# Splitting the weights of w_in again in the second and third pass, instead of storing them split

## The chip, the core and the metric

One core of one Trainium2 chip. The metric is device time in microseconds (us) of one execution of the whole program. The names of the engines are those of the profile: PE multiplies matrices (PEld is its weight load), DVE is VectorE, ACT is ScalarE, POOL is GpSimd, SP is SyncE, which here only issues DMAs.

## The reference, cut to what matters

Three blocks follow each other: an attention with mixed heads, a dense layer with a gate, and a soft mixture of eight experts. The change lies in the middle one, on 1792 tokens, with d_model 768 and d_ff 2048:

```python
x = attn_out.transpose(0, 2, 1, 3).reshape(B * S, H * D)
h = x @ w_in
g = h - np.tanh(h)
x = (g @ w_out).astype(np.float32)
```

The third block takes logits x @ phi of 32 slots, a softmax over the tokens and one over the slots, and runs eight experts (w1 768x1024, w2 1024x768) on the slots.

## The kernel before, in words

The middle block is stage 1 of `moe_and_slots`. It goes over the tokens in four passes of 512, 512, 512 and 256 (`PASS`), and in each pass over 16 units of w_in: a unit is the 768x128 piece of w_in whose 128 columns of h are made at once. So there are 64 steps, t = 0 to 63; step t belongs to pass t // 16 and unit t % 16. `LAST` is 48 (first step of the fourth pass), `HALVES` is 52, `THREE` is 54.

**The product.** `product(t)` (line 845) runs, for each of six slices c of 128 rows of d_model, three matmuls of 128x512: high part of w by high part of x, low part of w by high part of x, high part of w by low part of x. Each operand is kept as two numbers, a rounded high part and the remainder, so that three fast matmuls give nearly full float32 precision. A unit thus lies in SBUF as 128 x 2 x 2 x 384 floats (768 KB): index 1 is the half of d_model, index 2 is high (0) or low (1). The ring of units has four places, `unit(t)`; `load_w(t + 3)` is issued by SP at the start of step t and waits until the place is free, that is until product t - 1 has been read.

**Where the split comes from.** `split_w(t)` makes the two parts from an unsplit unit (384 KB, loaded into the place of the low part): ACT copies it rounded to the high part (line 792), then POOL subtracts this from it (line 793). In pass 1 (t below 16) all units come this way, from the DRAM scratch `wi`. `save_w(t)` then stores the split unit, 768 KB, to the DRAM scratch `wis` (line 806; from the ACT queue for t above 1). From t = 16 to t = 51, `load_w` fetches the split unit from `wis` (line 783), and neither ACT nor POOL does anything for it. From t = 52 on, units are loaded unsplit in two halves and split by `split_half` (lines 799 to 802).

**The gate.** `gate_act(t - 1)` is emitted at the start of step t. On ACT it makes, in this order, sq (line 865, from the product's PSUM bank hp), qd (866), then whatever is passed as `beside`, then g (871, tanh) and mk (872). `gate_first(t - 1)` and `gate_last(t - 1)` are five DVE operations: 876, 877, 884, 889 and 890, the last of which completes g. `turn_g(t - 2)`, hooked in front of slice c = 2 of product t, transposes the finished g of step t - 2 on PE (line 916, four matmuls), and ACT copies the result out (919, shown as quad or tq). Every fourth step, `logits` adds eight matmuls after the product (line 1000). Steps 1 to 5 of a pass also carry the slot softmax of the pass before: among others `gates_first` (three DVE operations, then an ACT exponential in line 1054) and `slot_sum` (16 matmuls, line 1082), which reads what 919 copied. In steps 8 to 13 of passes 2 and 3, `split_x` splits the next pass's tokens, one slice per step: an ACT copy (828) and a DVE subtraction (829).

**Queues.** The order is written out by hand, and each engine runs its instructions in that order. SP issues nearly all DMAs; the stores of line 806 are in the ACT queue between the ACT operations of a step. In pass 1 the steps also turn w_out (969, with copies 973 and 975), fold it with phi (981 to 991) and convert the last pieces of w_out from float64 on ACT, DVE and POOL (lines 50 to 71).

After pass 4 the experts follow, whose weights (1536 KB and parts of it) are loaded as places become free in the steps of passes 2 and 4 and after.

Of the kernel before, what the change touches and what calls it, by code (L numbers as in the profile page):

```python
# [9 lines left out]
FP32 = mybir.dt.float32  # L10
# [637 lines left out]
def moe_and_slots(tc, ident, xd, wi, wo, wo4, wis, consts, w1, w2, out, box):  # L648
    nc = tc.nc
    NT, DM = out.shape  # L650
    KD = DM // 128
    NF = len(wi)
# [23 lines left out]
    LAST = NST - NF  # L676
    THREE = LAST + 6
    HALVES = LAST + 4
# [11 lines left out]
    def bank(tag, shape, name):  # L690
        return bank_pool[tag].tile(shape, FP32, tag=tag, name=name)

    def r32(ap):
        return ap.bitcast(F32R)
# [12 lines left out]
    def unit(t):  # L707
        return ring[t % 4] if t < THREE else ring[(4, 0, 1)[(t - THREE) % 3]]
# [67 lines left out]
    def load_w(t):  # L776
        if t == THREE:
            ring.append(mem["tmp"].tile([128, RU], FP32, tag="gl", name="rg").rearrange(
                "p (m h i) -> p m h i", m=2, h=2))
        if t < NF or t >= HALVES:  # L780
            nc.sync.dma_start(out=unit(t)[:, :, 1], in_=wi[t % NF].rearrange("p (m i) -> p m i", m=2))
        else:
            nc.sync.dma_start(out=unit(t), in_=wis[t % NF])
# [3 lines left out]
            nc.sync.dma_start(out=unit(t)[:, m, 1], in_=wi[t % NF][:, m * HALF:(m + 1) * HALF])  # L787

    def split_w(t, eng):
        if t < NF:  # L790
            w = unit(t)
            nc.scalar.activation(out=r32(w[:, :, 0]), in_=w[:, :, 1], func=ACTF.Copy)
            eng.tensor_tensor(out=r32(w[:, :, 1]), in0=w[:, :, 1], in1=w[:, :, 0], op=ALU.subtract)  # L793

    def split_half(t, m):
        if HALVES <= t < NST:
            h, l = unit(t)[:, m, 0], unit(t)[:, m, 1]
            if m == 0:
                nc.vector.tensor_copy(out=r32(h), in_=l)  # L799
            else:  # L800
                nc.scalar.activation(out=r32(h), in_=l, func=ACTF.Copy)
            nc.gpsimd.tensor_tensor(out=r32(l), in0=l, in1=h, op=ALU.subtract)  # L802

    def save_w(t):
        if t < NF:
            (nc.scalar if t > 1 else nc.sync).dma_start(out=wis[t], in_=unit(t))

    def x_of(p, c, l):
# [42 lines left out]
    def temps_of(t):  # L851
        n = PASS[t // NF]
        if t < 2:
            part = [quad[:, i * n:(i + 1) * n] for i in range(4)]
            return part[0], part[1], part[2], part[3] if t else mem["g0"]
        i = (t - LAST) % 2 * n if t >= LAST else 0
        qd = mem["qe"] if t == LAST - 1 else mem["qd"]
        return mem["sq"][t], qd[:, i:i + n], mem["mk"][:, :n], g_of(t)

    def gate_act(t, beside=None):  # L860
        hp = hps[t]
        if t > 1:
            mem["sq"] = {t: bank(f"q{t % 2}", [128, PASS[t // NF]], "sq")}
        sq, qd, mk, g = temps_of(t)
        nc.scalar.activation(out=sq, in_=hp, func=ACTF.Square)  # L865
        nc.scalar.activation(out=qd, in_=sq, func=ACTF.Square, bias=tshift)
        if t >= LAST - 2:
            gate_poly(t)
        if beside:
            beside()  # L870
        nc.scalar.activation(out=g, in_=hp, func=ACTF.Tanh)
        nc.scalar.activation(out=mk, in_=sq, func=ACTF.Relu, bias=tlimit, scale=-1.0)  # L872

    def gate_poly(t):
        sq, qd, mk, g = temps_of(t)
        nc.vector.scalar_tensor_tensor(out=qd, in0=qd, scalar=TG_E, in1=sq, op0=ALU.add, op1=ALU.mult)  # L876
        nc.vector.scalar_tensor_tensor(out=qd, in0=sq, scalar=-TG_A, in1=qd, op0=ALU.add, op1=ALU.mult)
# [55 lines left out]
    def late_high(i):  # L933
        return mem["ex"][6].bitcast(I32).rearrange("p (n f) -> p n f", f=CV)[:, i]
# [26 lines left out]
    def load_o(f):  # L961
        if f < LATE:
            nc.sync.dma_start(out=mem["wo"][f % NG], in_=wo[f])
# [136 lines left out]
    def step(t):  # L1100
        b, f = divmod(t, NF)
        hooks = {}

        def on(c, fn, *a):
            hooks.setdefault(c, []).append(lambda: fn(*a))

        if t == LAST:
            mem["qe"] = keep.tile([128, TM], FP32, tag="et", name="qe")
        if 2 < t < THREE - 2:
            load_w(t + 3)  # L1110
        elif t >= THREE - 2:
            on(KD // 2, load_half, t + 3, 0)
            on(KD, load_half, t + 3, 1)
        for n, hf in pieces.get(t - 1, []):
            if hf:
                load_o(n + NG)
        if t > 2:
            split_half(t + 1, 0)
            gate_act(t - 1, lambda: split_half(t + 1, 1) if t >= NF else split_w(t + 1, nc.gpsimd))
        else:  # L1120
            split_w(t + 1, nc.gpsimd)
        u = t - 2
        ws = pieces.get(t, [])
        if ws:
            on(1, turn_w, *ws[0], 4 <= t <= len(late_w) + 4)
        if t > 2:
            on(1, gate_first, t - 1)
        on(5 if t == LAST + 1 else 4 if t > LAST + 2 else 2, turn_g, u)
        if ws:
            on(3 if t in folds else 5, turn_w, *ws[1], 4 <= t <= len(late_w) + 4)  # L1130
        if b == 0:
            on(1, save_w, t)
        if b and f == 1:
            on(3 if b < NPASS - 1 else 5, logits, b - 1, NQ - 1)
            on(4 if b < NPASS - 1 else 5, logits_out, b - 1)
        if b and f == 2:
            hooks[1] = [lambda: mix_t(b - 1), lambda: slot_exp(b - 1)] + hooks[1]
            on(3, mix_n, b - 1)
            on(KD, slot_run, b - 1)
            on(KD, gates_first, b - 1)  # L1140
        if b and f == 3:
            on(4, slot_turn, b - 1)
            on(KD, gates_last, b - 1)
        if b == NPASS - 1 and f in (3, 4):
            on(KD, slot_sum, b - 1, 2 * f - 6, 2 * f - 4)
        elif 0 < b < NPASS - 1 and f in (4, 5):
            on(3, slot_sum, b - 1, 2 * f - 8, 2 * f - 6)
        if t > 2:
            on(4, gate_last, t - 1)
        if 0 <= t - 2 < len(late_w):  # L1150
            late_load(t - 2)
        if 0 <= t - 4 < len(late_w):
            on(3, f64_abs, nc, late_high(t - 4), late_raw(t - 4))
            on(5, late_first, t - 4)
        if 0 <= t - 5 < len(late_w):
            on(5, late_last, t - 5)
        if 0 <= t - 6 < len(late_w):
            on(5, late_store, t - 6)
        if b + 1 < NPASS:
            if f == 6:  # L1160
                load_x(b + 1)
            if 8 <= f < 8 + KD:
                on(4, split_x, b + 1, f - 8, nc.vector if b else nc.gpsimd)
        if len(ws) > 2:
            on(KD - 1, turn_w, *ws[2])
        if t in folds:
            on(KD - 1, fold_first)
            on(KD, fold_last, folds[t])
        if u % NG == NG - 1 and u % NF < NF - 1:
            on(KD, logits, u // NF, u % NF // NG)  # L1170
        product(t, hooks)
        if b == 1 and f % 2 == 1 and f // 2 < NX:
            give(mem["ex"][f // 2], f // 2 == NX - 1)
        if b == 1 and f == NF - 1:
            give(mem["thp"].tile([128, EXB], FP32, tag="x1", name="ex"))
        if b == NPASS - 2 and f == NF - 1:
            mem["slow"] = True
            for l in range(2):
                give(xap.tile([128, EXB], FP32, tag=f"x{l}", name="ex"))
        if b == NPASS - 1:  # L1180
            if f == 3:
                give(rgp.tile([128, EXB], FP32, tag="rgs", name="ex"))
            if f == 4:
                firsts.close()
                zp = whole.enter_context(tc.tile_pool(name="m_z", bufs=1, reuse_waits="tile"))
                for i in range(2):
                    give(zp.tile([128, EXB], FP32, tag=f"z{i}", name="ex"))
            if f == NF - 2:
                load_piece(len(pending))
                give(rgp.tile([128, EXB], FP32, tag="rg", name="ex"))  # L1190
            load_piece(2 if f < 4 or f > NF - 3 else 1)
# [57 lines left out]
    for t in range(2, NST):  # L1249
        step(t)  # L1250
    t = NST
# [226 lines left out]
def fused_kernel(  # L1478
# [14 lines left out]
    nc = tc.nc  # L1493
    const = ctx.enter_context(tc.tile_pool(name="const", bufs=1))
    dram = ctx.enter_context(tc.tile_pool(name="xdram", bufs=1, space=bass.MemoryType.DRAM))
    ident = const.tile([128, 128], FP32, name="ident")
    make_identity(nc, ident)
    DM, FF = moe_w_in.shape
# [1 line left out]
    wi = [dram.tile([128, DM], FP32, tag=f"wi{f}", name=f"wi{f}") for f in range(FF // 128)]  # L1500
    wo4 = [dram.tile([128, 4 * DM], FP32, tag=f"wo{k}", name=f"wo{k}") for k in range(FF // 512)]
    wo = [wo4[f // 4][:, f % 4 * DM:(f % 4 + 1) * DM] for f in range(FF // 128)]
    wis = [dram.tile([128, 2, 2, DM // 2], FP32, tag=f"wis{f}", name=f"wis{f}") for f in range(FF // 128)]
    order = [(f, hf, o) for f in range(FF // 128) for hf in range(2) for o in range(2)]
    NSL = moe2_phi.shape[1]
    NG = 128 // NSL
# [62 lines left out]
```

## Time and profile before

| | us |
|---|---|
| runs shown: median (lowest to highest) | 881.85 (880.51 to 899.1) |
| the profiled execution's own time | 884.14 |
| its span, from the first to the last instruction | 882.4 |

| engine | busy us | share of the span |
|---|---|---|
| PE | 810.1 | 92% |
| ACT | 573.2 | 65% |
| DVE | 551.8 | 63% |
| POOL | 249.5 | 28% |

The DMAs move 224.53 MB in that execution (36.18 MB of them written to HBM). Stage 1 lies between about 440 and 774 us: pass 1 to 549, pass 2 to 639, pass 3 to 724, pass 4 to 774. A row of a timeline gives start, duration, engine, line, operation, what it writes and reads, a count, and in brackets how long the engine was idle before it and what ended that. A row of a group gives busy time, the mean of one in ns, and the idle time before them with what ended it.

### The profile page before, as it was taken

To read this page: it belongs to the slowest core of one execution; us is meant where nothing else is said; L and a number is where in the kernel's file an instruction comes from. 1 tells how busy PE (TensorE), PEld (TensorE's weight loads), DVE (VectorE), ACT (ScalarE), POOL (GpSimd) and SP (SyncE) were. 2 spreads that over 40 slices of the span, in tenths; PEclk is the share of its full clock that TensorE was granted. 3 is DMA by queue.
4 is the path that set the end of the run, shared out by engine and by line. 5 is a ranking of instruction groups with operands and counts; after the bars stand their busy time and mean duration, and the time that the engine had idled before them with its cause. 6 is when DMAs were issued, how large, how long until landed. Compare 5 with 4: busy or idle time off the path is not lost.

```text
span 882.4 us, 28630 instructions
## 1 busy us (share of the span) xinstructions
PE 810.1 (92%) x11780; PEld 578.4 (66%) x11780; DVE 551.8 (63%) x1168; ACT 573.2 (65%) x1358; POOL 249.5 (28%) x428
## 2 busy tenths in 40 slices
PE   8888998799888999999899999999999999999975
PEld 6456776577655776666676677667776786964422
DVE  5356766668756777888456975567765777830104
ACT  4686877778877788888666786546664666821103
POOL 5233343434433444454312552000000003700000
PEclk9899999999999999999999999999999999999988
DMA  9697788887898888885759985678755457999998
GB/s 178 180 223 212 199 240 232 228 222 202 231 242 232 226 224 248 247 251 188 245 195 355 348 292 214 221 308 319 292 215 178 147 186 255 308 348 415 424 393 316
DMA packets 131766, 224.53 MB, mean 254 GB/s; under 512 B 44852, under 2 KB 112436, under 8 KB 128052
## 3 DMA queue, kind: packets, MB, share of 16 engines
q1 hardware_dynamic: 129360, 211.68, 76.1%
q10 hardware_dynamic: 2276, 11.02, 3.1%
q8 instruction: 93, 1.52, 0.7%
q14 instruction: 37, 0.30, 0.1%
HBM read 147.96 MB, written 36.18 MB: 209 GB/s over the span
## 4 chain that ended last, share of the span: by engine, by line
PE 59%; DMA 17%; ACT 10%; DVE 7%; issue 4%; POOL 1%; SPq 0%; ACTq 0%; POOLq 0%; DVEq 0%
PE hp L845 21%; PE pm L313 7%; DMA D<-S 7%; DMA ex<-in_moe_w_dram 6%; PE vx L395 6%; PE sc L279 5%; PE tm L356 5%; ACT e L325 4%; DVE mx L317 3%; PE kx L236 2%; PE gt L916 2%; PE sp L1082 1%; ACT aT L370 1%; PE lgp L1000 1%; DVE xs L405 1%
## 5 line engine op out<-in xcount | busy, mean ns | idle before, releaser
L325 ACT ACTIVATE e<-pm,mx 128x448 f32<-128x448 f32 x184 | 116.2, 645 | 78.2 <-DVE mx L317 76.5
L317 DVE TENSOR_REDUCE mx<-pm 128x1 f32<-128x448 f32 x184 | 106.1, 618 | 81.2 <-PE pm L313 80.8
L845 PE MATMUL hp<-xa,rg 128*128 128x512 f32 x576 | 153.5, 407 | 2.2 <-POOL rg L793 2.2
L356 PEld LDWEIGHTS tm<-wk,e 64*56 64x56 f32 x5888 | 107.1, 130 | 51.8 <-issue 32.3
L313 PE MATMUL pm<-D,wpre 64*64 64x448 f32 (+1 forms) x736 | 112.5, 585 | 16.7 <-DMA D<-S 13.0
L845 PEld LDWEIGHTS hp<-xa,rg 128*128 128x128 f32 x576 | 103.2, 190 | 32.3 <-issue 10.5
L356 PE MATMUL tm<-wk,e 64*56 64x60 f32 x5888 | 110.6, 217 | 9.6 <-issue 9.0
L279 PE MATMUL sc<-khi,qT 64*120 64x448 f32 (+1 forms) x384 | 85.1, 397 | 14.6 <-DVE xs L405 10.3
L342 POOL TENSOR_SCALAR wk<-wpost,rv 128x60 f32<-128x60 f32 x184 | 89.7, 521 | 16.5 <-DVE rv L335 11.0
L287 ACT ACTIVATE S<-sc 120x448 f32<-120x448 f32 (+1 forms) x186 | 89.4, 566 | 5.5 <-PE sc L279 4.9
L395 PE MATMUL vx<-aT,vn 128*64 128x120 f32 (+1 forms) x1536 | 85.4, 265 | 2.0 <-ACT S L287 1.4
L331 POOL TENSOR_SCALAR rv<-ss 128x2 f32<-128x2 f32 x92 | 23.7, 258 | 223.3 <-ACT e L325 188.9
L802 POOL TENSOR_TENSOR rg<-rg 128x384 fp32r<-128x384 f32 x24 | 23.9, 1015 | 208.6 <-DVE rg L799 203.9
L876 DVE SCALAR_TENSOR_TENSOR qd<-qd,sq 128x512 f32<-128x512 f32 (+1 forms) x61 | 37.6, 617 | 69.9 <-ACT mk L872 64.7
L395 PEld LDWEIGHTS vx<-aT,vn 128*64 128x64 f32 x1536 | 75.9, 139 | 7.3 <-ACT S L287 3.6
L370 ACT ACTIVATE aT<-tm 128x480 f32<-128x480 f32 x144 | 76.2, 598 | 1.1 <-PE tm L356 1.1
L845 PE MATMUL hp<-xb,rg 128*128 128x512 f32 x288 | 74.7, 404 | 0.0
L865 ACT ACTIVATE sq<-hp 128x512 f32<-128x512 f32 (+1 forms) x62 | 32.9, 531 | 59.3 <-PE hp L845 59.2
L279 PEld LDWEIGHTS sc<-khi,qT 64*120 64x120 f32 (+1 forms) x384 | 46.8, 176 | 32.2 <-PE tm L356 10.8
L845 PEld LDWEIGHTS hp<-xb,rg 128*128 128x128 f32 x288 | 52.0, 188 | 16.6 <-issue 6.3
L71 POOL TENSOR_TENSOR fa<-fa,f 128x384 f32<-128x384 f32 x56 | 57.5, 1027 | 5.4 <-DVE f L66 1.1
L313 PEld LDWEIGHTS pm<-D,wpre 64*64 64x64 f32 (+2 forms) x736 | 25.6, 135 | 50.3 <-DMA D<-S 18.5
(197 smaller groups left out, 1399.9 us busy)
## 6 DMA issues: line engine op xcount, KB each, us to landing
ex<-in_moe_w_dram SPq DMA_DIRECT2D x21, 1536.0 KB
D<-S SPq DMA_DIRECT2D x144, 210.0 KB
rg<-wis SPq DMA_DIRECT2D x36, 768.0 KB
f<-in_moe_w_in_dram SPq DMA_DIRECT2D x32, 384.0 KB
wis<-rg ACTq DMA_DIRECT2D x14, 768.0 KB
f<-in_moe_w_out_dram SPq DMA_DIRECT2D x24, 384.0 KB
rg<-wi SPq DMA_DIRECT2D x19, 384.0 KB
wi<-fa SPq DMA_DIRECT2D x32, 192.0 KB
```

Source lines behind the costliest of these rows:

```text
L71: eng.tensor_tensor(out=out, in0=bits(a), in1=bits(p), op=ALU.add)
L279: nc.tensor.matmul(xs[e][0][:ni], lhsT=qT[n][s, l, p, :ni], rhs=kt[s], start=(i == 0), stop=(i == 2))
L287: nc.scalar.activation(out=dst, in_=xs[e][0][:ni], func=ACTF.Copy)
L313: nc.tensor.matmul(xs[x][64 * i:64 * i + 64], lhsT=wpre[k0:k1], rhs=d[i][k0:k1], start=True, stop=True)
L317: nc.vector.tensor_reduce(out=mx[:, x:x + 1], in_=xs[x], op=ALU.max, axis=AX.X, negate=True)
L325: nc.scalar.activation(out=es[x], in_=xs[x], func=ACTF.Exp, bias=mx[:, x:x + 1], accum_out=ss[:, x:x + 1])
L342: nc.gpsimd.tensor_scalar(out=wk, in0=wpost, scalar1=rv[:, x:x + 1], scalar2=None, op0=ALU.mult)
L356: nc.tensor.matmul(xs[i][64 * z:64 * z + JH, x, c], lhsT=es[x][h, j:j + JH], rhs=wks[x][h], start=True, stop=True)
L370: nc.scalar.activation(out=out[:, :, c0:c0 + m].rearrange("p a (x i) -> p a x i", x=2), in_=x, func=ACTF.Copy)
L395: nc.tensor.matmul(x[64 * e:64 * e + 64, i, :ni], lhsT=nat_v[b, h // NP][:, h % NP, c, :], rhs=a[:, c, h, :ni], start=(c == 0), stop=(c == ...
L845: nc.tensor.matmul(hp, lhsT=r32(w[:, m, hl, cs]), rhs=r32(x_of(b, c, l)), start=(c == 0 and i == 0), stop=(c == KD - 1 and i == 2))
L876: nc.vector.scalar_tensor_tensor(out=qd, in0=qd, scalar=TG_E, in1=sq, op0=ALU.add, op1=ALU.mult)
```

## The change

`load_w` fetches the unsplit 384 KB from `wi` for all steps below 48 (and from 52 on, as before); only steps 48 to 51 still fetch 768 KB from `wis`. `split_w` splits every unit below 48; in steps 15 to 46 it is what `gate_act` takes as `beside`, with POOL for the subtraction. `save_w` stores units 0 to 3 alone.

```diff
@@ load_w
-        if t < NF or t >= HALVES:
+        if t < LAST or t >= HALVES:
             nc.sync.dma_start(out=unit(t)[:, :, 1], in_=wi[t % NF].rearrange("p (m i) -> p m i", m=2))
         else:
             nc.sync.dma_start(out=unit(t), in_=wis[t % NF])
@@ split_w
-        if t < NF:
+        if t < LAST:
             w = unit(t)
             nc.scalar.activation(out=r32(w[:, :, 0]), in_=w[:, :, 1], func=ACTF.Copy)
             eng.tensor_tensor(out=r32(w[:, :, 1]), in0=w[:, :, 1], in1=w[:, :, 0], op=ALU.subtract)
@@ save_w
-        if t < NF:
+        if t < HALVES - LAST:
             (nc.scalar if t > 1 else nc.sync).dma_start(out=wis[t], in_=unit(t))
@@ step
-            gate_act(t - 1, lambda: split_half(t + 1, 1) if t >= NF else split_w(t + 1, nc.gpsimd))
+            gate_act(t - 1, lambda: split_half(t + 1, 1) if t >= LAST else split_w(t + 1, nc.gpsimd))
@@ fused_kernel
-    wis = [dram.tile([128, 2, 2, DM // 2], FP32, tag=f"wis{f}", name=f"wis{f}") for f in range(FF // 128)]
+    wis = [dram.tile([128, 2, 2, DM // 2], FP32, tag=f"wis{f}", name=f"wis{f}") for f in range(4)]
```

## Rows read from the trace of the kernel before

**Rows 1.** Windows by stage: stretch, us, busy time (instructions) per engine, granted clock, DMA share, GB/s

```profile
440.00:549.00 109.00, 103.30 (x680) 77.40 (x680) 75.74 (x132) 77.04 (x146) 39.42 (x27) 0.99 0.81 286
549.00:639.00 90.00, 89.53 (x458) 64.35 (x457) 59.71 (x99) 52.05 (x95) 0.00 (x0) 1.00 0.74 282
639.00:724.00 85.00, 84.87 (x432) 62.20 (x431) 58.80 (x100) 49.35 (x93) 0.00 (x0) 1.00 0.51 177
...
774.00:882.00 108.00, 88.47 (x743) 43.67 (x741) 21.77 (x58) 20.07 (x45) 2.32 (x8) 0.94 0.98 386
```

**Rows 2.** Timeline of pass 3, steps 39 to 41, ACT, DVE and PE

```profile
680.07 0.58 ACT L865 ACTIVATE sq<-hp 128x512 f32<-128x512 f32 x1 [2.16 <-PE hp L845]
...
681.23 0.60 PE L916 MATMUL gt<-ident,g 128*128 128x128 f32 x4
...
682.47 0.69 DVE L876 SCALAR_TENSOR_TENSOR qd<-qd,sq 128x512 f32<-128x512 f32 x1 [2.38 <-ACT mk L872]
...
684.62 0.58 ACT L865 ACTIVATE sq<-hp 128x512 f32<-128x512 f32 x1 [1.69 <-PE hp L845]
...
685.12 0.73 DVE L890 COPY_PREDICATED g<-mk,hp 128x512 f32<-128x512 int32 x1
...
686.00 0.63 PE L916 MATMUL gt<-ident,g 128*128 128x128 f32 x4
...
690.57 0.61 PE L916 MATMUL gt<-ident,g 128*128 128x128 f32 x4
```

**Rows 3.** Timeline of PE in pass 3, the transposes of steps 42 to 45

```profile
696.36 0.60 PE L916 MATMUL gt<-ident,g 128*128 128x128 f32 x4
...
700.91 0.60 PE L916 MATMUL gt<-ident,g 128*128 128x128 f32 x4
...
705.69 0.63 PE L916 MATMUL gt<-ident,g 128*128 128x128 f32 x4
...
710.27 0.60 PE L916 MATMUL gt<-ident,g 128*128 128x128 f32 x4
```

**Rows 4.** Timeline of pass 1, steps 10 to 12, where the split is made

```profile
511.72 1.84 POOL L793 TENSOR_TENSOR rg<-rg 128x768 fp32r<-128x768 f32 x1 [0.81 <-ACT rg L792]
...
516.31 0.58 ACT L865 ACTIVATE sq<-hp 128x512 f32<-128x512 f32 x1 [0.20 <-PE hp L845]
...
517.51 0.83 ACT L792 ACTIVATE rg<-rg 128x768 fp32r<-128x768 f32 x1
...
519.44 0.69 DVE L876 SCALAR_TENSOR_TENSOR qd<-qd,sq 128x512 f32<-128x512 f32 x1 [1.21 <-ACT mk L872]
```

**Rows 5.** Timeline of pass 2 around the slot softmax, steps 19 and 20

```profile
569.78 0.31 ACT L1054 ACTIVATE ceK<-ceK 128x128 f32<-128x128 f32 x1 [2.71 <-DVE ceK L1053]
...
575.04 0.74 DVE L890 COPY_PREDICATED g<-mk,hp 128x512 f32<-128x512 int32 x1
...
576.08 0.60 PE L916 MATMUL gt<-ident,g 128*128 128x128 f32 x4
...
577.79 0.62 PE L1082 MATMUL sp<-quad,es 128*32 128x512 f32 x2 [0.41 <-ACT quad L919]
```

**Rows 6.** Waits of SP's queue from 427 to 549 us: us in total, times, longest

```profile
SPq L781 <- DMA wis<-rg: 38.0, 9, 11.0
```

**Rows 7.** Timeline of pass 1, steps 8 and 9, ACT and PE

```profile
498.44 0.60 ACT L919 ACTIVATE quad<-gt 128x512 f32<-128x512 f32 x1 [0.93 <-DMA rg<-wi]
...
503.82 0.55 PE L969 MATMUL wt<-ident,ex 128*128 128x128 f32 x3 [0.59 <-ACT ex L973]
```

**Rows 8.** Timeline of pass 1: one DVE operation beside POOL and without it

```profile
500.24 1.28 POOL L829 TENSOR_TENSOR xb<-xb 128x512 fp32r<-128x512 f32 x1
...
500.56 1.17 DVE L54 TENSOR_SCALAR ex<-ex 128x384 f32<-128x384 f32 x1
...
516.03 0.34 DVE L54 TENSOR_SCALAR ex<-ex 128x384 f32<-128x384 f32 x1
```

**Rows 9.** One line, L829, subtraction of split_x: ns min/median/max, first and last start

```profile
L829 DVE TENSOR_TENSOR xa<-xa x12: 667/679/691, 438.4 to 629.4; 128x512 fp32r<-128x512 f32 x12
```


## Prediction

> **What bounds the kernel now.** I read the windows by stage first. In passes 2 and 3, the two stretches that the change alters most, PE is busy nearly all the time, 89.5 of 90 us and 84.9 of 85, at a granted clock of 1.00, POOL does nothing at all, and DMA is at 0.74 and 0.51 of its engines' time [rows 1]. So there is time on POOL, and DMA is not what these passes wait for; but a busy PE does not show how near the other engines are. For that I read the timeline of three plain steps of pass 3 [rows 2]. One product's gate goes: sq starts on ACT at 680.07, DVE's first operation (876) at 682.47, released by ACT's last one, mk (872), not by the qd that it reads; the last (890) ends at 685.12 + 0.73 = 685.85, and the transposes of this g start on PE at 686.00. Those transposes come two steps after the product that they belong to. The transposes of step 39 start at 681.23; then PE does the rest of product 39, whose sq starts at 684.62; so from one step's transposes to those two steps later there is a loop of 3.39 us (PE) + 5.93 us (680.07 to 686.00) = 9.32 us, and measured, 681.23 to 690.57, 9.34 us. PE's own work between two transposes is 4.55 us in a plain step (700.91 - 696.36) and 5.79 us where logits follow (696.36 - 690.57) [rows 2, 3]. Two plain steps are 9.10 us, less than 9.34: the loop over ACT and DVE already ends last once in four steps, and PE ends last in the others.
>
> That is the rule of this kernel: T(t), the start of the transposes in step t, is the later of T(t-1) + 4.55 (5.79 after logits) and T(t-2) + 9.34. From T(41) = 690.57 it gives 696.36, then 700.91, then 696.36 + 9.34 = 705.70 and 700.91 + 9.34 = 710.25; the rows have 705.69 and 710.27 [rows 2, 3]. Four steps are 19.70 us, 0.26 more than PE's work of 3 x 4.55 + 5.79 = 19.44.
>
> **The change part by part.**
>
> *The copy on ACT* (32 of them, steps 15 to 46) goes between qd and g, ahead of mk, which releases DVE. Pass 1 shows this very order: sq at 516.31, the copy at 517.51 for 0.83, and 876 at 519.44, again released by mk [rows 4]. From sq to 876 that is 3.13 us, against 2.40 in pass 3 [rows 2]. So a copy puts 0.73 us into the loop, and 9.34 becomes 10.07. What hides it is the slack of PE's bound, which is there in most steps. With T(41) = 0 the rule now gives 5.79; then 10.34 by PE (10.07 by the loop); then 15.86 by the loop (14.89 by PE); then 20.41 by both. Four steps are 20.41, 0.71 more than 19.70. So it costs 0.73 once where the loop ends last, not in every step. Walking through the 32 steps like this, there are five such places in the plain stretches: the transposes of steps 24, 28 and 32 in pass 2 and of 40 and 44 in pass 3. 5 x 0.73 = 3.65 us. If no slack hid it the price would be 32 x 0.73 = 23.4 us, and if DVE were not held by mk it would be 0; I take the walk, since its rule gives the rows of before to 0.02 us.
>
> *The steps around the slot softmax* have more PE work and mostly room for 0.73. There is one place in each pass where the delay counts twice: the exponential of 1054 waits on ACT for DVE, which does its part after 890, and the next sq stands behind it on ACT (569.78, idle 2.71 for DVE; there are two such rows, one in each pass) [rows 5]. A 890 that is 0.73 late makes that sq 0.73 late, and its gate gets a copy of its own: 1.46. In pass 2 the transposes of step 20 have 0.15 to spare (890 ends at 575.78, they start at 576.08, and 0.15 is the least gap in rows 2), so they come 1.31 later; but the slot sums behind them wait 0.41 for ACT in any case [rows 5], which takes about 0.4 back: 0.9. In pass 3, step 36, I find no such wait and no slack: 1.46. Together 2.4 us.
>
> *The subtraction on POOL*: 1.84 us, released by the copy [rows 4]. It ends 1.20 + 0.83 + 1.84 = 3.87 after sq, and the product that needs it starts at about the next sq, 4.55 later (684.62 - 680.07) [rows 2]. 0.7 us to spare, on an engine that was idle: nothing. If that cover went, each 0.1 us over would cost PE 0.1 us in that step. Bounds: 0, and, if all of PE's idle time in pass 1, 109.00 - 103.30 = 5.7 us [rows 1], were waits for the 13 subtractions that POOL makes there, 0.44 each, 32 x 0.44 = 14 us; I take 0, since the rows show when each one ends.
>
> *The loads* of units 16 to 47 halve, from 768 to 384 KB, 12.6 MB in all. SP issues them at the same places, two steps before ACT's copy reads them (before: three steps before PE did). Two steps are at least 9.1 us. What is queued ahead is at most one expert piece of 1536 KB, about 4 us at the 386 GB/s of the last stretch [rows 1]. They land in time, and nothing ended later for them in passes 2 and 3: 0 both ways. A copy whose load were late would hold tanh and mk behind it, and with them DVE and PE.
>
> *The stores* of units 4 to 15 go, 9.4 MB. In pass 1 SP's loads waited 38.0 us in nine waits for stores to leave a place of the ring [rows 6]. These loads are issued three steps early, so most of that is hidden. What I can follow to PE is one place: ACT idle for 0.93 before 498.44, the store in its queue waiting for a DMA, and PE then waiting 0.59 for ACT's copy in the next step [rows 7]. I take 0.7 us back. Bounds: 0, and all of PE's idle time there, the 5.7 us. I stay near the low end because the rest of that time includes waits on work that no store touches.
>
> *Pass 4 and after* are not edited. Their loads begin with the events of step 47, and from 774 us DMA is at 0.98 [rows 1]; a delay at step 47 is passed on whole, not absorbed, because these loads cannot start sooner.
>
> **Sum**: 3.65 + 2.4 - 0.7 = +5.3 us. The profiled execution took 884.14 us, its span 882.4 and 1.7 around it, and would become 889.4. It lies 2.3 us above the median of the runs shown, 881.85; from that median I predict 887.2 us (+0.6%).
>
> [...] In pass 1 DVE's line 54 took 1.17 us while POOL's line 829 ran (500.24 to 501.52), and ended 0.21 after it; alone it took 0.34 [rows 8]. [...]
>
> **The rivals.**
> 1. *Fewer bytes win.* SP's 38 us of waits were holding pass 1 more than I can follow, and all of PE's 5.7 us there go; this equals the loop's price of 6.0 less 0.3, so the time is about 882 (881.85 + 6.0 - 5.7), and about 876 if DVE were released before mk as well. For it: DMA is the only resource that gets lighter. Against it: passes 2 and 3 show no wait for DMA, and in pass 1 the same order of ACT held 876 to mk [rows 4]. It decides from 6 us of relief on: then not slower. Chance 0.16.
> 2. *The loop in every step.* If PE's bound gives less slack than the rule says, 32 x 0.73 - 0.7 = +22.7: 904.6. Against it: the rule gives the two rows that it was not read from to 0.02. Chance 0.04.
> 3. *POOL before DVE.* 829 runs 0.68 us in each of six steps of pass 2, and shorter, on half the columns, in six of pass 3 [rows 9]. It follows 890, so starts 0.73 + 5.78 = 6.51 after its step's sq, 0.7 to 1.96 after the next sq; POOL wants to start 2.03 after it. [...] Were POOL first, 829 would end 3.87 + 0.68 = 4.55 after sq and the 876 due at 3.13 would be 1.4 late: 12 x 1.4 = 17 us at most, 904 with the forecast. Chance 0.06.
> 4. *The change does less than it says*, for instance a unit still fetched split: 881.85. Nothing speaks for it. Chance 0.01.
>
> **How the numbers follow.** The forecast has 0.73. Its own range is 884 to 891, from the two ends of pass 1's gain that seem near and a repeat of the runs. For 8 in 10 it reaches down to the mild form of rival 1 and up to half of rival 3: 881 to 894. About 2% either way (864 and 899.5) is what a measurement of this kernel can tell from no change: faster than that 0.01, within 0.93, slower 0.06, from the full forms of rivals 2 and 3.
>
> **What would show it.** In the changed profile: 202.5 MB by DMA (224.53 - 12.6 - 9.4); line 792 48 times; in passes 2 and 3, 3.13 from sq to 876 in place of 2.40; transposes two steps apart by 10.07 where the loop ends last, four steps in 20.4; passes 2 and 3 together 6 us longer, pass 1 somewhat shorter, pass 4 and the tail as long as before. I am wrong if PE waits for POOL's 793 in passes 2 and 3, if 876 starts before mk ends, if DVE's 829 grows to over 2 us, if pass 1 loses more than 2 us, or if the tail changes its length.

## The result, and the profile after

The changed kernel takes 893.08 us (median of 6 runs), the kernel before, run beside it, 882.54 us (6 runs): a ratio of 1.0145, 95% interval 1.0101 to 1.019. The ratio is taken from fast runs alone, without the slowest of the kernel before, so it is above the quotient of the two medians, 1.0119. The change is thus inside 2%, but clearly a loss: 10.5 us by the medians (8.9 to 16.8 by the interval) where 5.3 were forecast. The time is inside the range of 881 to 894, outside the forecast's own 884 to 891. The profiled execution of the changed kernel took 888.63 us, with a span of 886.9.

The two profiled executions differ by only 4.5 us. A part of that lies ahead of the change: the first matmul of step 0 begins at 439.75 us before and at 436.01 after (from 431.64 to 440.10 in the profiles of all the kernels of this study), and steps 0 to 2 take 19.60 and 18.07 us; of the six profiled kernels built on the changed one three show the shorter value and three the longer. The granted clock tells the two apart. Windows from the first matmul of step 0, before and after (columns as in [rows 1]):

```profile
439.75:443.25 3.50, 3.50 (x39) 2.48 (x38) 1.77 (x3) 3.18 (x8) 0.00 (x0) 0.51 0.83 280
```

```profile
436.01:439.51 3.50, 3.50 (x79) 2.77 (x75) 1.76 (x3) 3.43 (x10) 0.00 (x0) 1.00 0.72 251
```

At a granted clock of 0.51 the first six matmuls of line 845 took 2.87 us together, at 1.00 they took 1.65. All nine profiles in which steps 0 to 2 take 19.6 us show this stretch, and none of the three in which they take 18.1; the change does not decide it. So I compare stretches, from the first matmul of a step (line 845) to the first one of a later step:

| stretch | before, us | after, us | difference | forecast |
|---|---|---|---|---|
| pass 1, steps 3 to 15 | 89.42 | 88.16 | -1.26 | -0.7 |
| passes 2 and 3, steps 16 to 47 | 175.01 | 186.75 | +11.74 | +6.05 |
| pass 4 | 50.70 | 50.53 | -0.17 | 0 |
| after pass 4 | 107.90 | 107.36 | -0.54 | 0 |

Within passes 2 and 3 the 11.7 us lie so: 6.9 in the plain stretches (forecast 3.65), 1.80 in step 20 and 2.18 in step 36 (forecast 0.9 and 1.46), 0.74 in step 16 (forecast 0). Four plain steps take 21.16 us in pass 2 and 21.07 in pass 3, against 19.83 and 19.68 before.

The page of the changed kernel, busy time of each engine and the DMA's volume:

```profile
PE 807.4 (91%) x11780; PEld 575.4 (65%) x11780; DVE 552.6 (62%) x1168; ACT 595.3 (67%) x1390; POOL 307.4 (35%) x460
...
DMA packets 134134, 202.51 MB, mean 228 GB/s; under 512 B 44660, under 2 KB 120436, under 8 KB 130420
```

The volume is the forecast one. The windows of passes 2 and 3 (columns as in [rows 1]):

```profile
542.00:637.00 95.00, 90.05 (x457) 63.93 (x456) 59.37 (x99) 63.22 (x111) 29.54 (x16) 1.00 0.55 199
637.00:729.00 92.00, 86.61 (x434) 62.23 (x433) 61.55 (x102) 60.00 (x107) 27.66 (x15) 1.00 0.34 108
```

DMA's share fell from 0.74 and 0.51 to 0.55 and 0.34, POOL has work now, and PE is idle for 4.95 and 5.39 us, where before it was idle for 0.5 and 0.1 [rows 1]. What PE waited for in these two passes (us in total, times, longest):

```profile
PE gt L916 <- DVE g L890: 5.6, 10, 0.8
PE gt L916 <- ACT qd L866: 2.4, 2, 1.2
PE sp L1082 <- ACT quad L919: 0.9, 1, 0.9
PE wt L969 <- DVE ex L975: 0.8, 1, 0.8
PE hp L845 <- POOL rg L793: 0.6, 1, 0.6
```

Together 10.3 us; before, the same view has one row, the 0.4 us for quad of [rows 5]. Ten of the waits are the transposes' for DVE's 890, the end of the gate. So in the plain stretches the gate is late ten times, not five: steps 24, 28, 32, 40 and 44, which the prediction named, are 0.53 to 0.73 us longer than before, and the step behind each (25, 29, 33, 41 and 45) another 0.62 to 0.69. Why, ACT's waits of the same stretch say:

```profile
ACT qd L866 <- DVE hp L889: 9.4, 16, 1.6
```

Line 866 writes qd, and there is one qd buffer: it must wait until line 889 of the previous gate has read it. Before, no such wait exists. But the trace of before shows how near it was. Timeline of the kernel before, pass 3, between the gates of [rows 2]:

```profile
680.68 0.69 ACT L866 ACTIVATE qd<-sq,tshift 128x512 f32<-128x512 f32 x1
...
684.40 0.69 DVE L889 SCALAR_TENSOR_TENSOR hp<-qd,hp 128x512 f32<-128x512 f32 x1
684.62 0.58 ACT L865 ACTIVATE sq<-hp 128x512 f32<-128x512 f32 x1 [1.69 <-PE hp L845]
685.23 0.69 ACT L866 ACTIVATE qd<-sq,tshift 128x512 f32<-128x512 f32 x1
```

889 is done at 685.09; 866 starts 0.14 later, on ACT's account alone, right behind sq. With some 0.09 from 889's end to an 866 that waits for it (693.30 to 693.39 below), qd could come round in 685.09 - 680.68 + 0.09 = 4.50 us, against a plain step of 4.55 on PE: 0.05 us of slack, which no wait shows. The changed kernel in pass 3, steps 41 to 44:

```profile
692.62 0.68 DVE L889 SCALAR_TENSOR_TENSOR hp<-qd,hp 128x512 f32<-128x512 f32 x1
693.33 0.73 DVE L890 COPY_PREDICATED g<-mk,hp 128x512 f32<-128x512 int32 x1
693.39 0.69 ACT L866 ACTIVATE qd<-sq,tshift 128x512 f32<-128x512 f32 x1 [0.41 <-DVE hp L889]
...
693.98 0.84 ACT L792 ACTIVATE rg<-rg 128x768 fp32r<-128x768 f32 x1
694.21 0.63 PE L916 MATMUL gt<-ident,g 128*128 128x128 f32 x4 [0.49 <-DVE g L890]
...
697.84 0.68 DVE L889 SCALAR_TENSOR_TENSOR hp<-qd,hp 128x512 f32<-128x512 f32 x1
...
698.62 0.69 ACT L866 ACTIVATE qd<-sq,tshift 128x512 f32<-128x512 f32 x1 [0.41 <-DVE hp L889]
...
703.39 0.58 ACT L865 ACTIVATE sq<-hp 128x512 f32<-128x512 f32 x1 [1.49 <-PE hp L845]
...
706.52 0.69 DVE L876 SCALAR_TENSOR_TENSOR qd<-qd,sq 128x512 f32<-128x512 f32 x1 [1.68 <-ACT mk L872]
```

From one 866 to the next, 693.39 to 698.62, is 5.23 us = 4.50 + 0.73. The copy lies inside this loop as it lies inside the transposes' loop, but this one closes in one step, the other in two: two rounds of qd are 10.46, more than the 10.07 of the transposes, so after the change qd ends last where plain steps follow each other. It makes the gate late in two of four steps; then the step with logits, 5.79 us on PE against 5.23, takes the delay up. Where 866 does not wait, sq to 876 is 3.13 (703.39 to 706.52), the forecast value.

With both loops in the rule (T(t), and the start of each 866 no earlier than 5.23 after the last one) four plain steps come to 21.08 by calculation; measured 21.07.

### The profile page after: what moved, and what is told of

It is laid out like the page before. It is cut to its first block, busy times and chain, and to the rows that moved or that the text cites. A ratio compares the mean times of both kernels' runs of the same rounds, so it can differ in the third digit from the quotient of the medians.

```text
span 886.9 us, 28736 instructions
## 1 busy us (share of the span) xinstructions
PE 807.4 (91%) x11780; PEld 575.4 (65%) x11780; DVE 552.6 (62%) x1168; ACT 595.3 (67%) x1390; POOL 307.4 (35%) x460
## 2 busy tenths in 40 slices
DMA packets 134134, 202.51 MB, mean 228 GB/s; under 512 B 44660, under 2 KB 120436, under 8 KB 130420
## 4 chain that ended last, share of the span: by engine, by line
PE 52%; DMA 14%; DVE 13%; ACT 12%; issue 6%; POOL 2%; SPq 0%; POOLq 0%; ACTq 0%; DVEq 0%
PE hp L845 14%; PE pm L313 7%; PE vx L395 7%; DMA ex<-in_moe_w_dram 6%; DMA D<-S 5%; PE sc L279 5%; PE tm L356 5%; DVE mx L317 3%; ACT e L325 3%; PE kx L236 3%; ACT rg L792 2%; PE gt L916 2%; PE sp L1082 1%; PE lgp L1000 1%; ACT S L287 1%
## 5 line engine op out<-in xcount | busy, mean ns | idle before, releaser
L793 POOL TENSOR_TENSOR rg<-rg 128x768 fp32r<-128x768 f32 x45 | 83.0, 1844 | 166.6 <-ACT rg L792 117.1
L313 PE MATMUL pm<-D,wpre 64*64 64x448 f32 (+1 forms) x736 | 110.5, 573 | 12.2 <-DMA D<-S 8.1
L71 POOL TENSOR_TENSOR fa<-fa,f 128x384 f32<-128x384 f32 x56 | 57.5, 1027 | 5.8 <-DVE f L66 1.5
L313 PEld LDWEIGHTS pm<-D,wpre 64*64 64x64 f32 (+1 forms) x736 | 25.3, 133 | 45.7 <-DMA D<-S 16.1
```

Of the source, the lines that this page charges most:

```text
L71: eng.tensor_tensor(out=out, in0=bits(a), in1=bits(p), op=ALU.add)
L313: nc.tensor.matmul(xs[x][64 * i:64 * i + 64], lhsT=wpre[k0:k1], rhs=d[i][k0:k1], start=True, stop=True)
```

## The experiments

Theory: the copy on ACT makes the loss, by the qd loop. Rivals: the transposes' loop alone; POOL's subtraction; the loads and stores. Ratios are to the kernel before, run beside it on the same chip.

**e2_copy_only and e3_pool_only**: the copy alone, and the subtraction alone, in the kernel before, each where the changed kernel has it (in e3 `beside` holds the second pair of lines in place of the first).

```diff
+    def beside(t):
+        if NF <= t < LAST:
+            h = r32(unit(t)[:, :, 0])
+            nc.scalar.activation(out=h, in_=bits(h), func=ACTF.Copy)
...
+            l = r32(unit(t)[:, :, 1])
+            nc.gpsimd.tensor_tensor(out=l, in0=bits(l), in1=unit(t)[:, :, 0], op=ALU.subtract)
```

> The kernel before, with one ACT copy of 128x768 put where the change puts its copy, in steps 15 to 46: it copies the high part of the next unit onto itself, so nothing computed changes, POOL does nothing more and all loads and stores stay as before. Theory (two loops over ACT and DVE: the transposes two steps on, and qd, the one buffer that line 889 of a gate must have read before line 866 of the next gate may write it, which makes qd to qd 4.51 us before and 5.24 with a copy of 0.73): passes 2 and 3, from the first matmul of step 16 to that of step 48, take 187 us as after the change, against 175.0 before; four plain steps 21.1, with waits of line 866 for line 889. One loop alone, as I forecast: 181, four plain steps 20.4. Rival, POOL or the unsplit loads make the second half of the loss: about 181 here. The total is 11 to 13 us over before by the theory, 6 by the others.

Measured: 893.1 us (4 runs), ratio 1.0153, interval 1.0086 to 1.0221. Passes 2 and 3 take 185.81 us, four plain steps 21.15 and 21.07. The waits of ACT and PE there (line numbers 9 higher):

```profile
ACT qd L875 <- DVE hp L898: 9.0, 16, 1.3
...
PE gt L925 <- DVE g L899: 5.6, 10, 0.8
```

The same sixteen and ten waits as in the changed kernel. So the copy alone makes 10.8 of the 11.7 us.

> The kernel before, with one POOL subtraction of 128x768 per step in steps 15 to 46, of the shape and in the place of the change's, but no ACT copy and the loads and stores of before. The low part of a unit in passes 2 and 3 becomes low minus high, which changes the values of the products there and not their number. Theory: nothing, passes 2 and 3 take 175.0 us within 0.5 and the total is that of before. Rival, POOL beside DVE's line 829 or late for PE: up to 5 us more, waits of PE for POOL, 829 over 1 us.

Measured: 881.2 us (10 runs), ratio 0.9969, interval 0.9923 to 1.0016; passes 2 and 3 take 175.14 us, 0.13 more than before. POOL alone costs nothing, as forecast.

**e1_two_qd**: a second qd buffer in the changed kernel. It lies where another tile is free, so it serves the odd gates from the sixth of a pass on; gates 16 to 20 and 32 to 36 have one buffer as before.

```diff
+    def second(t):
+        return NF <= t < LAST - 1 and t % 2 and t % NF >= 5
...
-        qd = mem["qe"] if t == LAST - 1 else mem["qd"]
+        qd = mem["qe"] if t == LAST - 1 else mem["qd2"] if second(t) else mem["qd"]
...
+        if NF <= t < LAST and f == 6:
+            mem["qd2"] = keep.tile([128, TM], FP32, tag="et", name="qd")
```

> The changed kernel with a second qd buffer for the odd steps from the sixth step of passes 2 and 3 on, so that line 866 need not wait for line 889 of the gate before it. Theory: the waits of 866 for 889 go there, four plain steps take 20.4 in place of 21.1, passes 2 and 3 take 183 to 184 us in place of 186.8, the total 3 to 4 us less than the changed kernel. Rival (the qd wait only shifts what PE waits for anyway): 186 to 187.

Measured: 890.0 us (9 runs), ratio 1.0093, interval 1.0065 to 1.0122. Four plain steps take 20.57 and 20.42 us, and the waits in passes 2 and 3 are now

```profile
ACT qd L869 <- DVE hp L892: 2.7, 2, 1.6
...
PE gt L919 <- DVE g L893: 3.6, 5, 0.8
```

This is the cleanest piece of evidence. With the qd loop gone from the plain stretches, what is left is what the prediction walked through: five late gates in place of ten, four steps of pass 3 in 20.42 where 20.41 was forecast. They lie in the very steps that it named, 24, 28, 32, 40 and 44, each 0.71 to 0.76 us longer than before, 3.63 together (forecast 3.65). The forecast's rule was right for the loop it knew. Passes 2 and 3 fall by 3.3 us to 183.45; steps 20 and 36, where qd still has one buffer, stay at 8.96 and 8.97.

**e8_two_copies**: e2 with its copy made twice.

```diff
             nc.scalar.activation(out=h, in_=bits(h), func=ACTF.Copy)
+            nc.scalar.activation(out=h, in_=bits(h), func=ACTF.Copy)
```

> The kernel before with two copies of 128x768 on ACT in the place where the change puts one, in steps 15 to 46, each of the next unit's high part onto itself. Theory: with 1.46 us more the loop over qd is 5.97 us and longer than any plain step of PE, and now ends last in each: four plain steps take 23.9 us (19.7 before, 21.1 with one copy). The transposes' loop alone would give 21.6. Rival (a copy costs the same each time): 22.5.

Measured: 920.82 us (a single run). Four plain steps take 23.21, 24.41, 23.29 and 24.39 us, mean 23.8; the rule with both loops gives 23.9, with the transposes' loop alone 21.6, and the same price for each copy 22.5. Passes 2 and 3 are 34.4 us over before; 7.1 of these lie in step 20, where PE's granted clock was 0.50 over 6.80 us (last section). From one 866 to the next it is now 6.10 us (623.15 to 629.25), and four such rounds are 24.40, what the later fours take. The second copy adds 0.87 to the round, 3.5 in four steps, and 2.7 of these are paid: past its slack, the loop hands on most of what is put into it.

**e4_stores_kept**: the changed kernel with all sixteen units stored.

```diff
-        if t < HALVES - LAST:
+        if t < NF:
             (nc.scalar if t > 1 else nc.sync).dma_start(out=wis[t], in_=unit(t))
```

> The changed kernel with all 16 units stored as before (the twelve stores of pass 1 come back; nobody reads those twelve). Theory: steps 3 to 15, from the first matmul of step 3 to that of step 16, take 89.4 us as before, against 88.2 after the change, most of it in step 9 (11.7 against 10.8), where ACT's queue waits; passes 2 and 3 stay at 187. Rival (pass 1 is shorter by chance, or by what came before it): 88.2.

Measured: 896.02 us (a single run). Steps 3 to 15 take 89.39 us, as before the change (89.42). SP's waits for stores in pass 1, first in the changed kernel and then in this one:

```profile
SPq L781 <- DMA wis<-rg: 9.6, 3, 6.7
```

```profile
SPq L781 <- DMA wis<-rg: 42.5, 10, 10.9
```

Against 38.0 before [rows 6]. The stretch as a whole does not show that pass 1 gained by the stores, since its step 3 varies by itself: 6.60 us here, 7.60 before, 7.16 in the changed kernel, and 9.64 in e1, where the granted clock over the step was 0.82; with it e1, which lacks the stores too, takes 90.65 for steps 3 to 15. Step 9 does show it. It takes 10.84 to 10.87 us in the five profiled kernels without the twelve stores (the changed kernel, e1, e5, e6, e9) and 11.58 to 12.64 in the seven with them (11.67 before, 12.64 here), while steps 4 to 8 take 32.13 to 32.17 in all twelve. PE's wait of 0.59 for 973 of [rows 7] is gone from step 9 of the changed kernel. So the stores are worth 0.83 us between before and after; the other 0.44 of the 1.26, in step 3, is not shown to be theirs.

Passes 2 and 3 were expected to stay at 187; they take 189.97, 3.2 us more than in the changed kernel, all of it in steps 20 and 36; in step 20 PE's granted clock fell to 0.56 (last section).

**e5_copy_late**: the changed kernel, with copy and subtraction of unit t+2 issued at the end of step t, behind mk in place of ahead of it.

```diff
-            gate_act(t - 1, lambda: split_half(t + 1, 1) if t >= LAST else split_w(t + 1, nc.gpsimd))
+            gate_act(t - 1, lambda: split_half(t + 1, 1) if t >= LAST else split_w(t + 1, nc.gpsimd) if t < NF else None)
...
+        if t >= NF - 1:
+            on(5, split_w, t + 2, nc.gpsimd)
```

> The changed kernel with ACT's copy and POOL's subtraction moved: from step 15 on they are made for the unit after the next, and stand at the end of the step, behind mk and the copies of 919 and 828, so in neither loop. Theory (only the place of the copy costs, not its time on ACT): passes 2 and 3 take 175 us within 1, as before the change, four plain steps 19.7 to 19.8; pass 1 keeps its 1.2 us, so the total is 0 to 2 us under before. Rival (ACT's 0.83 us per step costs wherever it stands): 180 us or more for the two passes.

Measured: 881.88 us (12 runs), ratio 0.9991, interval 0.995 to 1.0033. Passes 2 and 3 take 175.85, four plain steps 19.84 and 19.69, and no qd wait is left. All copies, subtractions, loads and stores of the change are there; only the place of copy and subtraction differs, and e2 shows that the copy's is the one that counts. Step 16 stays at 9.22, since gate 15 keeps its old order.

**e6_poly_early and e7_before_poly**: the changed kernel, and the kernel before, with 876 and 877 issued right behind qd from gate 15 on, so that they no longer stand behind mk.

```diff
-        if t >= LAST - 2:
+        if t >= NF - 1:
             gate_poly(t)
```

> The changed kernel with the two DVE operations 876 and 877 of each gate from step 16 on emitted right behind qd and ahead of the copy, tanh and mk, as the kernel already does from the gate of step 46 on. Then 876 is released by qd, and the copy is beside DVE's work. Theory: both loops become shorter than PE's work (transposes to those two steps on 8.2 us against 9.1), four plain steps take PE's 19.45 in pass 3, passes 2 and 3 take 173 to 174 us in place of 186.8, and the total is 1 to 3 us under before. Rival (mk waits for 877, and 890 for mk, so the loop hardly shortens): 180 or more.

Measured: 881.28 us (12 runs), ratio 0.9993, interval 0.9959 to 1.0026. Four plain steps take 19.70 and 19.47 us, PE's own work (19.44 in the prediction). Passes 2 and 3 take 175.75, where 173 to 174 was expected. The order on ACT has a price of its own:

```profile
ACT mk L872 <- DVE qd L877: 9.1, 32, 1.0
...
PE sp L1082 <- ACT quad L919: 1.5, 1, 1.5
```

mk now waits for 877, and 919 stands behind mk; so step 20 takes 8.27 us, 1.1 more than before, and the slot sums wait.

> The kernel before with the same move of 876 and 877 as in the run with the early operations on the changed kernel, and no other edit. Theory: passes 2 and 3 take 173 to 174 us here too, since the copy is then hidden; the total is 1 to 2 us under before, and 1 us over the changed kernel with the same move, whose pass 1 is shorter. Rival (the copy still costs there): the two kernels differ by more than 2 us in passes 2 and 3.

Measured: 883.24 us (12 runs), ratio 1.0025, interval 0.9997 to 1.0053; passes 2 and 3 175.43, again over the expected 173 to 174, plain steps 19.70 and 19.47, step 20 8.25. The move gains 0.1 to 0.2 us in four plain steps and loses more in steps 20 (1.1) and 16 (0.4). The two kernels with it differ by 0.3 us in passes 2 and 3, so the copy is hidden there.

**e9_best and e10_before_best**: is there more to be had? e9 is the changed kernel with the late copy, the early polynomial from gate 16 on, and the first half of one step's slot sum moved back; e10 is the kernel before with the last two moves.

```diff
-        if t >= LAST - 2:
+        if t >= NF:
             gate_poly(t)
...
-            on(3, slot_sum, b - 1, 2 * f - 8, 2 * f - 6)
+            on(8 - f, slot_sum, b - 1, 2 * f - 8, 2 * f - 6)
```

The late copy of e9 is that of e5, from step 14 on.

> The changed kernel with three moves: tanh and DVE's polynomial stand right behind qd, ahead of mk, from gate 16 on; the copy and the subtraction for unit t+2 are issued at the end of step t, from step 14 on; and the first half of the slot sum of one step moves one place later in its step. My theory (the price is the loop over qd and the steps beside the softmax, all of which this takes away): passes 2 and 3 together 173.5 us (step 16 about 8.5, step 20 about 6.8, four plain steps 19.7 and 19.5, which is PE's own work), pass 1 1.2 shorter than before, so 2 to 3 us under the kernel before. Rival: what the moves give beside the softmax is lost again further on, as PE is the bound there anyway; then passes 2 and 3 stay near 175.7, and the time is that of the kernel before to 0.2%.

Measured: 880.16 us (12 runs), ratio 0.9987, interval 0.9952 to 1.0021; passes 2 and 3 175.30, steps 3 to 15 87.71.

> The kernel before with the early polynomial from gate 16 on and the moved half of the slot sum, so with the order of the run beside it but with split loads and all stores. My theory: halved loads are worth nothing in passes 2 and 3, so these take 173.5 us here too, and the run is 1 to 2 us under the kernel before; the other one is lower by the 1.2 us of pass 1 alone. Rival: halved loads do matter in passes 2 and 3; then the two differ there by over 2 us.

Measured: 877.95 us (12 runs), ratio 0.9976, interval 0.9937 to 1.0015; passes 2 and 3 174.30, steps 3 to 15 88.80.

The theory's 173.5 missed: step 20 takes 8.40 us in e9 and 7.55 in e10, not 6.8, and PE still waits there for quad, 1.6 and 0.8 us. Why the two differ in that step was not tried. Both ratios' intervals include 1, so no version here is shown to beat the kernel before. What the two do show: with split loads of twice the bytes passes 2 and 3 take no longer than with halved ones.

## Why the prediction was half right

**The bound**: right that PE has little slack and that a gate released late by mk is the copy's way to the end. The sentence that failed is "so it costs 0.73 once where the loop ends last, not in every step". It walks one loop, the transposes', which closes over two steps, and took the rest of PE's time as slack. The qd buffer closes a second loop in each step, with 0.05 us to spare. With it the price in the plain stretches is 6.9 us, not 3.65; without it, in e1, it is 3.63. That the rule gave the rows of before to 0.02 was no evidence against a second loop: at 4.50 under 4.55 it left no trace in them. The second rival (a price in every step) had the kind of it, for another reason; its 22.7 is far above, as the delay reaches PE in ten plain steps and in steps 16, 20 and 36, while PE's own work hides it in the others.

**The steps around the slot softmax**: direction right, size 2.4 in place of 3.98, plus 0.74 in step 16. Timeline of the changed kernel at step 20, against [rows 5]:

```profile
570.77 0.69 ACT L866 ACTIVATE qd<-sq,tshift 128x512 f32<-128x512 f32 x1 [1.10 <-DVE hp L889]
...
571.36 0.83 ACT L792 ACTIVATE rg<-rg 128x768 fp32r<-128x768 f32 x1
...
571.58 0.63 PE L916 MATMUL gt<-ident,g 128*128 128x128 f32 x4 [1.15 <-ACT qd L866]
...
573.14 0.60 ACT L919 ACTIVATE quad<-gt 128x512 f32<-128x512 f32 x1
...
573.79 0.62 PE L1082 MATMUL sp<-quad,es 128*32 128x512 f32 x2 [0.89 <-ACT quad L919]
```

The transposes are late, as forecast. But the slot sums' wait did not give 0.4 back; it grew from 0.41 to 0.89, since the copy stands on ACT ahead of 919 too. In step 16 DVE's 975 stands behind the later 890, and PE's transposes of the weight wait 0.8 us for it, the row "wt" above: a queue behind the waiting engine that the prediction did not follow. Step 36 is 1.34 from the copy (8.14 in e2, 6.80 before) and 0.84 from POOL, as follows.

**The subtraction on POOL**: forecast nothing, and e3 says nothing; but with the copy it costs 0.84 us in step 36. I expected the collision at 829, which kept its time in the changed kernel (670 to 693 ns in full width). In e3 it took up to 1.49 us in full width and up to 1.23 on half the columns (0.41 before), but passes 2 and 3 were only 0.13 us over before there: no run shows the third rival's 1.4 us in each of twelve steps. In the changed kernel the collision came at another operation. Changed kernel, steps 34 to 36:

```profile
651.49 1.82 POOL L793 TENSOR_TENSOR rg<-rg 128x768 fp32r<-128x768 f32 x1 [4.23 <-ACT rg L792]
651.65 1.68 DVE L1029 TENSOR_TENSOR nm<-nm,run_m 128x1 f32<-128x1 f32 x1
...
657.58 0.31 ACT L1054 ACTIVATE ceK<-ceK 128x128 f32<-128x128 f32 x1 [2.58 <-DVE ceK L1053]
...
659.90 1.84 POOL L793 TENSOR_TENSOR rg<-rg 128x768 fp32r<-128x768 f32 x1 [6.59 <-ACT rg L792]
...
661.79 1.43 PE L845 MATMUL hp<-xa,rg 128*128 128x512 f32 x5 [0.64 <-POOL rg L793]
```

and the same operation in e2, with no POOL beside it:

```profile
654.57 0.16 DVE L1038 TENSOR_TENSOR nm<-nm,run_m 128x1 f32<-128x1 f32 x1
```

A maximum of two columns takes 1.68 us in place of 0.16, and ends at 653.33, 0.02 after POOL. The 1.5 us go down the chain: 1054 is late, sq and the copy behind it too, and PE waits 0.64 for a subtraction. So "I am wrong if PE waits for POOL's 793 in passes 2 and 3" came true, once.

**The loads**: right; PE and ACT have no wait for DMA in passes 2 and 3, and e10 takes no longer there than e9.

**The stores**: mechanism, place and size right: 0.83 us in step 9 where 0.7 was taken. SP's waits fell from 38.0 to 9.6 us, so 28 us of waiting were worth 0.8. The first rival needed 6. The 0.44 that step 3 adds in the table is not shown to come from them.

**Pass 4 and after**: right, within 0.6 us. That the change does less than it says is out: 202.51 MB.

**Sum**: 6.9 + 0.1 spread over other steps + 3.98 + 0.74 - 1.26 = +10.5. That this is the difference of the medians to a tenth is in part luck: it leaves out steps 0 to 2 (19.60 us before and 18.07 after), and the ratio's interval is 8.9 to 16.8 us.

## What to carry to other kernels

Before adding work to an engine, list every buffer that the engine writes and that another reads, and for each work out the round from one write to the next against the bound: a loop that is 0.05 us short of it shows no wait in the trace, and ends last as soon as more than that is added. Here the loop that closes in one step doubled the late gates of the one that closes in two, from five to ten. And where such work has time to spare, as this copy, issue it behind what the others wait for: the place in the queue alone was worth 10.9 us in passes 2 and 3 (e5 against the changed kernel).

## What the runs showed of the hardware

**A VectorE operation on 128 elements took 1.68 us beside POOL, and 0.16 without it.** Of the profiled runs with the subtraction, 1029 began beside it in four: the changed kernel, e1, e4 (each 1.68 to 1.69 us) and e6. In e6 it began late in POOL's operation and took as long as was left of it:

```profile
644.21 1.83 POOL L793 TENSOR_TENSOR rg<-rg 128x768 fp32r<-128x768 f32 x1 [3.93 <-ACT rg L792]
...
645.47 0.58 DVE L1029 TENSOR_TENSOR nm<-nm,run_m 128x1 f32<-128x1 f32 x1
```

POOL ends at 646.04, DVE at 646.05. In e5 and e9 no subtraction lay beside it, in e3 only the last 0.14 us of one, and it took 0.16. The operation of DVE just before, 1027 (644.76, a maximum over 512 columns read from PSUM), lay wholly beside the same subtraction and took 0.68 us, against 0.69 without POOL in the kernel before (564.89). So of these two 1029 alone took longer; why it and not 1027, no run here shows.

**PE's granted clock fell to 0.56 behind a pause in e4, and stayed at 1.00 behind a like one in the changed kernel.** In e4, windows of 2 us around step 20 (PE, PEld, DVE, ACT, POOL busy, granted clock, DMA share, GB/s):

```profile
574.00:576.00 2.00, 0.87 (x6) 0.42 (x5) 1.93 (x5) 0.96 (x2) 0.00 (x0) 1.00 0.82 267
576.00:578.00 2.00, 1.17 (x7) 0.69 (x6) 0.99 (x4) 2.00 (x4) 1.47 (x1) 1.00 0.08 28
578.00:580.00 2.00, 1.94 (x12) 0.59 (x16) 1.97 (x4) 0.01 (x1) 0.35 (x1) 0.56 0.00 0
580.00:582.00 2.00, 2.00 (x10) 0.47 (x3) 0.91 (x2) 0.00 (x0) 0.00 (x0) 0.58 0.00 0
```

and in the changed kernel the stretch that answers to it:

```profile
570.00:572.00 2.00, 0.85 (x7) 0.45 (x6) 1.90 (x6) 1.23 (x2) 0.00 (x0) 1.00 0.69 209
572.00:574.00 2.00, 1.11 (x9) 0.59 (x11) 1.00 (x3) 1.74 (x4) 1.73 (x1) 1.00 0.00 0
574.00:576.00 2.00, 2.00 (x18) 0.56 (x11) 1.96 (x4) 0.00 (x0) 0.08 (x1) 1.00 0.00 0
```

PE was busy 2.04 of 4 us in the one and 1.96 in the other, with waits of 1.1 and 0.9 us in both. In e4 the granted clock was then 0.56 and 0.58 in the next two windows, and step 20 took 10.60 us in place of 8.96; step 36 took 10.56. In the changed kernel the clock stayed at 1.00, and step 20 of e1 and e2 took 8.97 as there. What tells them apart no run here shows. In e8 the waits of step 20 were longer (2.88 and 1.77 us), and behind them the granted clock was 0.50:

```profile
583.45:590.25 6.80, 5.78 (x21) 2.44 (x22) 3.31 (x5) 0.97 (x2) 0.00 (x0) 0.50 0.01 2
```

So steps 20 and 36, in which the copy makes PE wait, took 1.6 us more each in e4 than in the changed kernel. That the waits brought the clock down is not shown, and whether this is behind the spread of the changed kernel's times (888.63 to 901.84) was not tried.
